# A two-layer decode step streamed through one 26 MB buffer: cache tiles of 4 MB, softmax rows turned in place, other places for the weights

## The chip, the cores and the metric

One core of a Trainium2 chip runs the kernel. Its engines are TensorE (PE), VectorE (DVE), ScalarE (ACT), GpSimd (POOL) and SyncE (SP), and 16 DMA engines bring data from the chip's main memory. The metric is the device time of one execution in microseconds (us); the kernel before took a median of 853.35 us in three runs (853.08 to 855.14).

## What is computed

Two transformer layers for one new token of each of 8 batches, in float32. Both layers use the same weights and the same caches:

```python
x = A_x                                    # (8, 1, 1024)
for layer in range(2):
    x = x + attention(layernorm(x))        # q = x @ wq: 32 heads of 128
    x = x + mlp(layernorm(x))              # gelu(x @ w1 + b1) @ w2 + b2, 3584 hidden
# attention: 4 K/V heads, each for 8 query heads, 4096 cached positions:
# softmax(q @ k.T * 128 ** -0.5) @ v, all heads joined, @ wo
```

The K cache holds 8 MB for each batch and so does V (4 heads x 4096 positions x 128 x 4 bytes), which makes 128 MB that each layer reads. wq and wo are 16 MB each, w1 and w2 are 14 MB each.

## The kernel before, in words

**One buffer.** Nearly everything that comes from memory lands in one tile, the arena: 52 units of 1024 columns (SCW) over 128 partitions, which is 512 KB a unit and 26 MB in all. A transfer of k units takes k neighbouring units from a given place. Sizes and places below are in units: (8, 28) is a 4 MB transfer into units 28 to 35. A piece of the cache, the half of one K/V head's positions of one batch, is 2 units (1 MB), so a batch has 8 pieces of K and 8 of V.

**One queue.** All these transfers stand in the list `stream`, in the order in which they are wanted, and SP issues them in that order and no other (`pump`, L229; the issue is L236). The head of the list is issued when its units are free. `release` frees a tile's units after its last reader and pumps. In the built program the wait is SP's: the transfer waits until PE has finished the last matmul that read the old content of these units, and all later transfers stand behind it. The 16 DMA engines work such transfers off one after the other; each is cut into rows of one partition, so every engine carries a sixteenth of each. A tile is one transfer with one semaphore, so PE can start on a 4 MB tile only when all of it has landed.

**Layer 0.** Units 0 to 27 hold wq, 14 MB of which stay for layer 1 (`held`, pieces ("q", kt, u)); the last 2 MB go partly to PSUM (`park`) and to the tile `spare`, and 64 KB are fetched once more ("qe"). Units 28 to 47 are the ring for the caches: 20 units. For each batch, PE multiplies the queries with 8 pieces of K (`scores`, L512: 4 matmuls of 512 columns for a piece, which the profile counts as 8), DVE scales the result into a row and takes maxima (L517), `probs` (L526 to L535) makes the exponentials on ACT, `turn` (L544 to L550) transposes them on PE, and `values` (L568) multiplies them with 8 pieces of V, after which `heads` (L580) joins each K/V head's result. PE does this in order: no V piece before its batch's softmax. The row of a batch and its transposed form S lie in the two units OWN = 50, 51 (`arena.own`).

**From layer 0 to layer 1.** The last 6 of the 8 pieces of batch 7's V stay in the arena, since layer 1 starts with batch 7 (`kept`). Then wo (`project`, L351), w1 (`expand`, L264, with `hidden_group` turning each group of h) and w2 (`swap`, L388) are streamed. wo and w1 of layer 0 go 4 units at a time through three places of 4 units (BLOCK_AT). In `swap`, w2 is multiplied in four column blocks c, and after each block two kt of wq, kept in units 0 to 27, make layer 1's queries (L299) and free their units. All of w2 but its last 4 of 28 kt in each block stays, in 24 units, for layer 1.

**Layer 1.** The batches go from 7 down to 0, with the 28 units that w2 leaves. At its end wo, w1 and the missing w2 are streamed again.

What sets the order is thus written by hand: sizes and places in the lists at L706 to L733. A place that is used again soon makes its transfer wait for PE.

Of the kernel before, what the change touches and what calls it, by code (L numbers as in the profile page):

```python
# [15 lines left out]
B, D = 8, 1024  # L16
HQ, HKV, SK, DH = 32, 4, 4096, 128
REP = HQ // HKV
F = 3584
# [34 lines left out]
class Arena:  # L54


    def __init__(self, ap):
        self.ap = ap
        self.freed = dict.fromkeys(range(N_UNIT), 0)
        self.clock = 0  # L60
        self.limit = OWN[0][0]
        self.own_at = OWN[0]

# [9 lines left out]
    def own(self):  # L73
        return self.take(1, self.own_at)

# [29 lines left out]
def decode_layers(ctx: ExitStack, tc: tile.TileContext, x, kc, vc, wq, wo, w1, w2, out):  # L105
# [123 lines left out]
    def pump():  # L229
        while stream:  # L230
            key, k, src, starts, keys = stream[0]
            slot = arena.take(k, [i for i in starts if i + k <= arena.limit])
            if slot is None:
                return
            stream.pop(0)
            nc.sync.dma_start(out=slot.ap[:, 0:src.shape[1]], in_=src)  # L236
            slot.cols = src.shape[1]
            slot.keys = keys
            held[key] = slot
# [155 lines left out]

    def arrive(c, kind):
        kts = W2_KTS[kind]
        slot = held[f"w2u{st['layer']}" if kind == "u" else "w2", c, *(() if kind == "u" else (kind,))]
        for e, kt in enumerate(kts):
            w2_at[c, kt] = slot.ap[:, e * Q4:(e + 1) * Q4]  # L400
        return list(kts)

    def swap():

        ys = small_ps("s")
        down(ys[:, 0:Q4], 0, arrive(0, 0), 0)
        flush()
# [13 lines left out]
        for c in range(CB):  # L421
            y = ys[:, c % 2 * Q4:(c % 2 + 1) * Q4]
            kts = []
            for kind in W2_ORDER[c]:
                kts += arrive(c, kind) if c or kind != 0 else []
            down(y, c, kts, NFT - len(kts))
            release(held.pop(("w2u0", c)))
            ysb = row_s[:, c % 2 * Q4:(c % 2 + 1) * Q4]
# [9 lines left out]
            for kt in (2 * c, 2 * c + 1):  # L438
                for u in range(2):
                    if kt < NT - 1:  # L440
                        late.append(lambda kt=kt, u=u: used(kt, u))
                        if (kt, u) != (3, 1):
                            late.pop()()
                    elif u == 0:
                        spot = st.pop("unparked")
                        q_part(acc, u, kt, 0, spot.ap)
                        spot.free()
                    else:
                        slot = held.pop(("qe", 0))
                        q_part(acc, u, kt, 0, slot.ap[:, 0:W - KEEP])  # L450
# [104 lines left out]
    def totals(b):  # L555
        pl = small_ps("pt")
        nc.tensor.matmul(pl[:, 0:HQ], ones, dl_s[b % 2], start=True, stop=True)
        nc.vector.reciprocal(rl_s[b % 2], pl[:, 0:HQ])
        st.pop(("row", b)).free()

# [86 lines left out]
    def unpark():  # L647
        spot = st.pop("spot")
        slot = arena.take(2, OWN[1][0:1])
        nc.scalar.activation(slot.ap, spot, AF.Copy)  # L650
        return slot
# [35 lines left out]
    any_of = lambda *at: lambda k, i: at  # L687

    def fixed(*at):
        return lambda k, i: (at[i],)  # L690

    def down_weights(c, layer, *spots):
        for kind, at in zip(W2_ORDER[c] if layer == 0 else "u", spots):
            key = (f"w2u{layer}", c) if kind == "u" else ("w2", c, kind)
            k0, k1 = (c * NFT + e for e in (W2_KTS[kind][0], W2_KTS[kind][-1] + 1))
            stream.append((key, (k1 - k0) // 4, w2[0][:, k0 * Q4:k1 * Q4], (at,), ()))

# [4 lines left out]
    def batch(layer, b, k_spots, v_spots):  # L702
        for a, spots in (("k", k_spots), ("v", v_spots)):
# [13 lines left out]
    i, j, k = LAST_BLOCKS  # L717
    down_weights(0, 0, i, j, j + 3)
    down_weights(1, 0, k, j + 2, 0)
    down_weights(2, 0, 2, 6, 1)  # L720
    down_weights(3, 0, 0, 8, 12)
    qe = (("qe", 0), 1, wq[0][:, -W:-KEEP], (1,), ())
    stream.append(qe)
    batch(1, last_b, ((4, 16), (4, 20), (4, 24), (2, 0), (2, 16)), ((4, 18),))
    batch(1, last_b - 1, ((2, 22), (4, 24), (2, 0), (2, 16), (4, 18), (2, 36)), ((8, 40), (8, 16)))
    cycle = [(((4, 24), (8, 36), (4, 44)), ((12, 16), (4, 36))), (((8, 40), (4, 16), (4, 20)), ((4, 24), (12, 36))),
             (((12, 16), (4, 36)), ((8, 40), (8, 16)))]
# [3 lines left out]
    weights(("i1",), w1[0], [4] * 6 + [2, 2], fixed(40, 44, 16, 20, 24, 36, 40, 42))  # L731
    for c in range(CB):
        down_weights(c, 1, 44 + c)  # L733
    pump()
    rs = layernorm(x_row, rsum)
    queries(rs)
    for layer in range(2):
        st["layer"] = layer
        b2_row = spare[:, 0:Q4]
        hooks = {("turn", last_b): opened} if layer == 0 else {  # L740
            ("v", *v_at(last_b - 2, 0)): lambda: bias_row(b2_row, spare[:, Q4:Q4 + CH]),
            ("v", *v_at(last_b - 1, 1)): rebuild}
# [7 lines left out]
        else:  # L750
# [24 lines left out]
            for c in range(CB):  # L775
                arrive(c, "u")
            grow(W2_KTS["u"], range(CB - 1))
            grow(W2_KTS["u"], (CB - 1,))
            nc.vector.tensor_tensor(x_row, x_row, y[0], ALU.add)
# [70 lines left out]
```

## Time and profile before

| | us |
|---|---|
| median of 3 runs (range) | 853.35 (853.08 to 855.14) |
| the profiled execution's own time | 854.68 |
| its span, first to last instruction | 852.9 |
| PE busy in it | 542.3 |
| DVE busy | 204.2 |
| ACT busy | 73.6 |

The queue of SP carries 358.82 MB, in 135 loads and one store. A row of the chain of waits gives a start, a length and what was worked or waited on; a DMA row in it begins with the issue of the transfer and ends when its tile has landed. A row of the timeline is start, duration, engine, line, operation and shapes, the count, and in brackets how long the engine had been idle before it and for what. PEclk is the clock granted to TensorE as a share of full speed. In a table of windows "DMA share" is the mean busy share of the 16 DMA engines.

### The profile page before, as it was taken

To read this page: it belongs to the slowest core of one execution; us is meant where nothing else is said; L and a number is where in the kernel's file an instruction comes from. 1 tells how busy PE (TensorE), PEld (TensorE's weight loads), DVE (VectorE), ACT (ScalarE), POOL (GpSimd) and SP (SyncE) were. 2 spreads that over 40 slices of the span, in tenths; PEclk is the share of its full clock that TensorE was granted. 3 is DMA by queue.
4 is the path that set the end of the run, shared out by engine and by line. 5 is a ranking of instruction groups with operands and counts; after the bars stand their busy time and mean duration, and the time that the engine had idled before them with its cause. 6 is when DMAs were issued, how large, how long until landed. Compare 5 with 4: busy or idle time off the path is not lost.

```text
span 852.9 us, 9923 instructions
## 1 busy us (share of the span) xinstructions
PE 542.3 (64%) x4226; PEld 190.8 (22%) x4226; DVE 204.2 (24%) x758; ACT 73.6 (9%) x164; POOL 1.7 (0%) x13
## 2 busy tenths in 40 slices
PE   0746665675765656655787786647557465474788
PEld 0212121121211121222233232111212111121344
DVE  0012231322222122300420242223223122231034
ACT  0110000000000000001311100000000000000042
POOL 0000000000000000000000000000000000000000
PEclk9977767776678777787889987858688777786889
DMA  9999999999999999999999999999999999999995
GB/s 400 417 442 417 438 427 436 422 440 420 429 428 431 433 435 424 426 427 428 423 388 407 416 433 422 438 425 445 434 419 424 434 425 443 423 425 442 415 426 241
DMA packets 19772, 359.60 MB, mean 422 GB/s; under 512 B 2192, under 2 KB 2576, under 8 KB 3600
## 3 DMA queue, kind: packets, MB, share of 16 engines
q1 hardware_dynamic: 19584, 358.82, 98.8%
q8 instruction: 33, 0.54, 0.3%
q10 hardware_dynamic: 144, 0.15, 0.1%
q14 instruction: 11, 0.09, 0.0%
HBM read 358.83 MB, written 0.13 MB: 421 GB/s over the span
## 4 chain that ended last, share of the span: by engine, by line
DMA 70%; PE 25%; DVE 2%; issue 1%; ACT 1%; another core or an unknown queue 1%; SPq 0%; ACTq 0%; DVEq 0%
DMA arena<-in_k_dram 27%; DMA arena<-in_v_dram 22%; DMA arena<-in_wo_dram 8%; DMA arena<-in_w_dram 8%; PE sps L512 7%; PE o_ps L568 7%; DMA arena<-in_wq_dram 5%; PE acc L264 2%; PE y L351 2%; PE sps L394 2%; PE sps L388 1%; PE acc L299 1%; PE sps L544 1%; PE sps L284 1%
## 5 line engine op out<-in xcount | busy, mean ns | idle before, releaser
L568 PE MATMUL o_ps<-arena 128*32 128x512 f32 x1024 | 166.9, 777 | 81.3 <-DMA arena<-in_v_dram 81.3
L512 PE MATMUL sps<-arena,qz 128*32 128x512 f32 x1024 | 152.2, 737 | 95.4 <-DMA arena<-in_k_dram 95.1
L512 PEld LDWEIGHTS sps<-arena,qz 128*32 128x32 f32 x1024 | 32.9, 127 | 179.5 <-DMA arena<-in_k_dram 95.8
L573 DVE SCALAR_TENSOR_TENSOR scr<-o_ps,bits,scr 128x128 f32<-128x128 f32 x192 | 67.4, 351 | 6.8
L535 ACT ACTIVATE arena<-arena,bits 128x512 f32<-128x512 f32 x32 | 22.8, 714 | 526.0 <-DVE scr L530 526.0
L568 PEld LDWEIGHTS o_ps<-arena 128*32 128x32 f32 x1024 | 33.6, 131 | 145.9 <-issue 110.0
L571 DVE TENSOR_SCALAR scr<-o_ps,bits 128x128 f32<-128x128 f32 x64 | 22.4, 351 | 171.1 <-PE o_ps L568 171.1
L351 PE MATMUL y<-arena,oxT 128*32 128x256 f32 x512 | 38.9, 459 | 32.0 <-DMA arena<-in_wo_dram 32.0
L517 DVE TENSOR_SCALAR_CACHE_REDUCE arena<-sps 128x512 f32<-128x512 f32 x32 | 22.1, 692 | 148.5 <-PE sps L512 148.5
L544 PE MATMUL sps<-ident,arena 128*128 128x128 f32 x128 | 29.3, 392 | 24.5 <-ACT arena L535 24.3
L264 PE MATMUL acc<-arena,oxT 128*32 128x256 f32 x448 | 35.4, 455 | 10.2 <-DMA arena<-in_w_dram 10.2
L580 PEld LDWEIGHTS sps<-bits,scr 128*128 128x128 f32 x128 | 21.7, 213 | 68.2 <-issue 40.1
L299 PE MATMUL acc<-arena,oxT 128*32 128x512 f32 (+1 forms) x250 | 32.1, 649 | 5.6 <-DMA arena<-in_wq_dram 4.1
L351 PEld LDWEIGHTS y<-arena,oxT 128*32 128x32 f32 x512 | 17.7, 127 | 51.5 <-DMA arena<-in_wo_dram 37.3
L581 DVE TENSOR_TENSOR oxT<-sps,scr 128x8 f32<-128x8 f32 x64 | 10.5, 164 | 72.8 <-PE sps L580 72.8
L544 PEld LDWEIGHTS sps<-ident,arena 128*128 128x128 f32 x128 | 21.2, 196 | 29.5 <-ACT arena L535 29.3
L580 PE MATMUL sps<-bits,scr 128*128 128x8 f32 x128 | 27.6, 288 | 0.0
L526 PE MATMUL sps<-scr,bits 128*128 128x128 f32 x32 | 7.7, 322 | 22.8 <-DVE scr L522 22.8
L264 PEld LDWEIGHTS acc<-arena,oxT 128*32 128x32 f32 x448 | 14.8, 125 | 22.7 <-DMA arena<-in_w_dram 9.7
L388 PE MATMUL sps<-arena,oxT 128*32 128x256 f32 x224 | 16.4, 423 | 4.2 <-DMA arena<-in_w_dram 4.2
L548 DVE COPY arena<-sps 128x512 f32<-128x512 f32 x16 | 11.1, 692 | 30.6 <-PE sps L544 30.6
L394 PE MATMUL sps<-arena,oxT 128*32 128x256 f32 x224 | 16.6, 394 | 0.8 <-DVE oxT L341 0.5
(109 smaller groups left out, 229.0 us busy)
## 6 DMA issues: line engine op xcount, KB each, us to landing
arena<-in_v_dram SPq DMA_DIRECT2D x19, 4096.0 KB, 18.9
arena<-in_k_dram SPq DMA_DIRECT2D x31, 2048.0 KB, 17.0
arena<-in_k_dram SPq DMA_DIRECT2D x12, 4096.0 KB, 18.7
arena<-in_w_dram SPq DMA_DIRECT2D x17, 2048.0 KB, 12.1
arena<-in_v_dram SPq DMA_DIRECT2D x4, 6144.0 KB, 25.6
arena<-in_v_dram SPq DMA_DIRECT2D x11, 2048.0 KB, 20.6
arena<-in_wo_dram SPq DMA_DIRECT2D x10, 2048.0 KB, 12.6
arena<-in_k_dram SPq DMA_DIRECT2D x2, 6144.0 KB, 23.5
```

The lines of the kernel that those rows point to most:

```text
L264: nc.tensor.matmul(acc[32 * j:32 * j + 32, 0:G], xnT[:, kt * XS:kt * XS + 32], slot.ap[:, c:c + G], start=(kt < 4), stop=(kt >= NT - 4))
L299: nc.tensor.matmul(acc[u][32 * j:32 * j + 32, d0 - j * CH:d1 - j * CH], xnT[:, kt * XS:kt * XS + 32], ap[:, d0 - c0:d1 - c0], start=(kt == ...
L351: nc.tensor.matmul(y[32 * j:32 * j + 32, 0:Q4], lhs[:, n * B:n * B + 32], slot.ap[:, c + j * Q4:c + (j + 1) * Q4], start=(n == 0), stop=(n ...
L388: nc.tensor.matmul(y[32 * g:32 * g + 32], h_at(kt), w2_at[c, kt], start=(n < 4), stop=(n >= NFT - 4))
L394: nc.tensor.matmul(y[32 * c:32 * c + 32], h_at(kt), w2_at[c, kt], start=(kt == 0), stop=(kt == NFT - 1))
L512: nc.tensor.matmul(ps[32 * g:32 * g + 32, :], qz[:, c:c + 32], kt[:, g * CH:(g + 1) * CH], start=(j == 0), stop=(j == HKV - 1))
L535: nc.scalar.activation(part, part, AF.Exp, bias=bias, scale=1.0, accum_out=ls[:, h:h + 1])
L544: nc.tensor.transpose(pp[:, t * P:(t + 1) * P], row[:, c:c + P], ident)
L568: nc.tensor.matmul(o[32 * g:32 * g + 32, :], s[:, g], v[:, g * CH:(g + 1) * CH], start=(half == 0), stop=(half == NH - 1))
L571: nc.vector.tensor_scalar(r, o[:, 0:P], sel_t[:, 0:1], None, op0=ALU.mult)
L573: nc.vector.scalar_tensor_tensor(r, o[:, t * P:(t + 1) * P], sel_t[:, t:t + 1], r, op0=ALU.mult, op1=ALU.add)
L580: nc.tensor.matmul(po[:, 0:REP], r_s[j % 2], sel_h, start=True, stop=True)
```

## The change

- **Rows turned in place.** `turn` writes S over the row itself, half by half, so one unit is enough: OWN is unit 51. In layer 1 that row lies in `spare` (`own_ap`), behind the 64 KB of wq that go to x_row now ("qe", with k = 0: no units).
- **7 of 8 pieces of batch 7's V stay**, so layer 1 loads one piece (1 MB) less.
- **4 MB cache tiles.** In layer 0, batches 1 to 6 load K as two tiles of 8 units and V as 4, 8 and 4 units. Both 4-unit tiles of V use units 44 to 47. In layer 1, batches 5 to 0 use 8-unit tiles alone, through three places (24, 32, 16).
- **10 places for wo and w1 of layer 0** (units 42 to 51): wo in tiles of 5 and 4 units by turns at 46 and 42, w1 in tiles of 4, 2 and 4 at 42, 50 and 46. Before it was three places of 4 units.
- **w2 in other parts** (W2_PARTS: kt and place); the last group of h is turned before w2 is begun (`swap` flushes first).

```diff
@@ constants
 N_UNIT = 52
-OWN = (50, 51), (14, 15)
-BLOCK_AT = 28, 32, 48
-LAST_BLOCKS = 28, 32, 48
+OWN = N_UNIT - 1
+UNPARK = 16
...
-W2_KTS = {0: range(16), 1: range(16, NFT - 4), "u": range(NFT - 4, NFT)}
-W2_ORDER = (0, 1, "u"), (0, 1, "u"), (0, 1, "u"), ("u", 0, 1)
+LAST = NFT - 4
+W2_PARTS = (((8, 48), (16, 42), (4, 50)), ((4, 51), (8, 46), (8, 0), (8, 2)),
+            ((4, 50), (16, 4), (8, 8)), ((4, 51), (16, 10), (8, 14)))
+LATE_AT = 40, 41, 50, 51
@@ class Arena
-        self.limit = OWN[0][0]
-        self.own_at = OWN[0]
+        self.limit = OWN
+        self.own_ap = None
...
     def own(self):
-        return self.take(1, self.own_at)
+        return self.take(1, (OWN,)) if self.own_ap is None else Kept(self.own_ap)
@@ def pump
-            slot = arena.take(k, [i for i in starts if i + k <= arena.limit])
+            if not k:
+                slot = Kept(starts)
+            else:
+                slot = arena.take(k, [i for i in starts if i + k <= arena.limit])
@@ def swap
         ys = small_ps("s")
-        down(ys[:, 0:Q4], 0, arrive(0, 0), 0)
         flush()
...
-            kts = []
-            for kind in W2_ORDER[c]:
-                kts += arrive(c, kind) if c or kind != 0 else []
-            down(y, c, kts, NFT - len(kts))
-            release(held.pop(("w2u0", c)))
+            n = 0
+            for i in range(len(W2_PARTS[c])):
+                kts = arrive(("w2", c, i), w2_kts(c, i))
+                down(y, c, kts, n)
+                n += len(kts)
+            release(held.pop(("w2", c, [m for m, _ in W2_PARTS[c]].index(4))))
...
-        arena.own_at = OWN[1]
+        arena.own_ap = spare[:, 0:SCW]
@@ def turn
         row = st["row", b].ap
-        st["S", b] = arena.own()
+        st["S", b] = st.pop(("row", b))
@@ def totals
-        st.pop(("row", b)).free()
@@ the lists of transfers
-    n_kept = 6
+    n_kept = 7
...
-    cycle = [(((8, 32), (4, 40), (4, 44)), ((8, 28), (8, 36))), (((4, 44), (8, 28), (4, 36)), ((8, 40), (8, 28))),
-             (((8, 36), (4, 44), (4, 28)), ((8, 32), (8, 40))), (((8, 28), (4, 36), (4, 40)), ((4, 44), (8, 28), (4, 36))),
-             (((8, 40), (4, 28), (4, 32)), ((8, 36), (4, 44), (4, 28)))]
-    for n, b in enumerate(orders[0][:-1]):
-        batch(0, b, *cycle[n % 5])
-    batch(0, last_b, ((8, 36), (4, 44), (4, 28)), ((4, 32), (8, 36), (4, 44)))
-    blocks = any_of(*BLOCK_AT)
-    weights(("o0",), wo[0], [4] * 8, blocks)
-    weights(("i0",), w1[0], [4] * (F // CH), blocks)
...
+    batch(0, 0, ((8, 36), (4, 44), (4, 32)), ((4, 28), (8, 36), (4, 44)))
+    for b in orders[0][1:-1]:
+        a, e = (28, 36) if b % 2 else (36, 28)
+        batch(0, b, ((8, a), (8, e)), ((4, 44), (8, a), (4, 44)))
+    batch(0, last_b, ((8, 28), (8, 36)), ((2, 44), (8, 28), (6, 36)))
+    weights(("o0",), wo[0], [5, 4, 5, 4, 5, 4, 5], fixed(46, 42, 46, 42, 46, 42, 46))
+    weights(("i0",), w1[0], [4, 2, 4, 4, 2, 4, 4, 2, 2], fixed(42, 50, 46, 42, 50, 46, 42, 50, 46))
...
-    qe = (("qe", 0), 1, wq[0][:, -W:-KEEP], (1,), ())
+    stream.append((("qe", 0), 0, wq[0][:, -W:-KEEP], x_row[:, 0:W - KEEP], ()))
-    batch(1, last_b, ((4, 16), (4, 20), (4, 24), (2, 0), (2, 16)), ((4, 18),))
-    batch(1, last_b - 1, ((2, 22), (4, 24), (2, 0), (2, 16), (4, 18), (2, 36)), ((8, 40), (8, 16)))
+    batch(1, last_b, ((4, 18), (2, 22), (4, 24), (2, 16), (2, 50), (2, 18)), ((2, 20),))
+    batch(1, last_b - 1, ((4, 22), (2, 26), (6, 16), (4, 28)), ((8, 32), (8, 16)))
...
-    for n, b in enumerate(orders[1][2:]):
-        batch(1, b, *cycle[n % 3])
-    weights(("o1",), wo[0], [4, 12, 8, 4, 2, 2], fixed(24, 36, 16, 24, 36, 38))
+    at = [24, 32, 16] * (4 * B)
+    for b in orders[1][2:]:
+        batch(1, b, *([(8, at.pop(0)), (8, at.pop(0))] for _ in "kv"))
+    weights(("o1",), wo[0], [8, 8, 8, 4, 2, 2], fixed(24, 32, 16, 24, 28, 30))
...
-        b2_row = spare[:, 0:Q4]
+        b2_row = spare[:, SCW:SCW + Q4]
```

The first place is SP's queue in layer 0, batches 1 and 2; 128x8192 is a tile of 8 units (4 MB), 128x4096 one of 4. Before:

```order
L236 DMA arena<-in_k_dram 128x4096
L236 DMA arena<-in_k_dram 128x8192
L236 DMA arena<-in_k_dram 128x4096
L236 DMA arena<-in_v_dram 128x8192 x2
L236 DMA arena<-in_k_dram 128x8192
L236 DMA arena<-in_k_dram 128x4096 x2
L236 DMA arena<-in_v_dram 128x8192 x2
```

After:

```order
L240 DMA arena<-in_k_dram 128x8192 x2
L240 DMA arena<-in_v_dram 128x4096
L240 DMA arena<-in_v_dram 128x8192
L240 DMA arena<-in_v_dram 128x4096
L240 DMA arena<-in_k_dram 128x8192 x2
L240 DMA arena<-in_v_dram 128x4096
L240 DMA arena<-in_v_dram 128x8192
L240 DMA arena<-in_v_dram 128x4096
```

K comes in two tiles instead of three, V in three instead of two; the two small V tiles share their place.

The second place is the same queue at the end of layer 0: the last cache tiles, wo, and the start of w1 (in_w stands for w1 and w2). Before:

```order
L236 DMA arena<-in_k_dram 128x4096 x2
L236 DMA arena<-in_v_dram 128x4096
L236 DMA arena<-in_v_dram 128x8192
L236 DMA arena<-in_v_dram 128x4096
L236 DMA arena<-in_wo_dram 128x4096 x8
L236 DMA arena<-in_w_dram 128x4096 x8
L236 DMA arena<-in_w_dram 128x2048
L236 DMA arena<-in_w_dram 128x1024
```

After:

```order
L240 DMA arena<-in_v_dram 128x2048
L240 DMA arena<-in_v_dram 128x8192
L240 DMA arena<-in_v_dram 128x6144
L240 DMA arena<-in_wo_dram 128x5120
L240 DMA arena<-in_wo_dram 128x4096
L240 DMA arena<-in_wo_dram 128x5120
L240 DMA arena<-in_wo_dram 128x4096
L240 DMA arena<-in_wo_dram 128x5120
L240 DMA arena<-in_wo_dram 128x4096
L240 DMA arena<-in_wo_dram 128x5120
L240 DMA arena<-in_w_dram 128x4096
L240 DMA arena<-in_w_dram 128x2048
```

The eight equal tiles of wo became seven of 5 and 4 units, and w1 got tiles of 2 units between those of 4.

The third place is PE at the start of `swap`: L284 (after: L288) turns groups of h, L388 (L392) is w2, L433 (L443) turns the block's result, and L299 (L303) is a kept piece of wq. Before:

```order
L264 MATMUL acc<-arena,oxT 32x256 x8
L284 MATMUL sps<-ident,scr 128x128 x2
L388 MATMUL sps<-arena,oxT 32x256 x16
L284 MATMUL sps<-ident,scr 128x128 x2
L388 MATMUL sps<-arena,oxT 32x256 x12
L433 MATMUL sps<-bits,scr 128x8 x2
L299 MATMUL acc<-arena,oxT 32x512 x16
```

After:

```order
L268 MATMUL acc<-arena,oxT 32x256 x8
L288 MATMUL sps<-ident,scr 128x128 x4
L392 MATMUL sps<-arena,oxT 32x256 x28
L443 MATMUL sps<-bits,scr 128x8 x2
L303 MATMUL acc<-arena,oxT 32x512 x16
```

The last turn of h moved ahead of the 16 matmuls of w2 that stood before it, and the block's 28 matmuls are one run.

More of the change, by code (lines that the diff above doesn't have):

```diff
@@ L394, in down_row, with w2_kts, arrive @@
                 nc.tensor.matmul(y[32 * c:32 * c + 32], h_at(kt), w2_at[c, kt], start=(kt == 0), stop=(kt == NFT - 1))
-    def arrive(c, kind):
-        kts = W2_KTS[kind]
-        slot = held[f"w2u{st['layer']}" if kind == "u" else "w2", c, *(() if kind == "u" else (kind,))]
+    def w2_kts(c, i):
+        if W2_PARTS[c][i][0] == 4:
+            return range(LAST, NFT)
+        k0 = sum(n for n, _ in W2_PARTS[c][:i] if n > 4)
+        return range(k0, k0 + W2_PARTS[c][i][0])
+    def arrive(key, kts):
+        slot = held[key]
         for e, kt in enumerate(kts):
-            w2_at[c, kt] = slot.ap[:, e * Q4:(e + 1) * Q4]
-        return list(kts)
+            w2_at[key[1], kt] = slot.ap[:, e * Q4:(e + 1) * Q4]
+        return kts
     def swap():
         ys = small_ps("s")
-        down(ys[:, 0:Q4], 0, arrive(0, 0), 0)
         flush()
@@ L449, in swap @@
                         slot = held.pop(("qe", 0))
[L450 removed]
+                        q_part(acc, u, kt, 0, slot.ap)
                         q_part(acc, u, kt, W - KEEP, spare)
@@ L648, in unpark @@
         spot = st.pop("spot")
-        slot = arena.take(2, OWN[1][0:1])
+        slot = arena.take(2, (UNPARK,))
         nc.scalar.activation(slot.ap, spot, AF.Copy)
@@ L734, in decode_layers @@
+    for c in range(CB):
+        down_weights(("late", c), c, range(LAST, NFT), LATE_AT[c])
     pump()
```

30 lines of the change are left out of this document (10 added, 20 removed).

## Prediction

> **What bounds the kernel now.** I read the page's line of the DMA engines and its chain, then a table of windows, then the chain row by row.
>
> ```profile
> DMA  9999999999999999999999999999999999999995
> DMA 70%; PE 25%; DVE 2%; issue 1%; ACT 1%; another core or an unknown queue 1%; SPq 0%; ACTq 0%; DVEq 0%
> ```
>
> ```profile
> core 0: us, PE busy (x) PEld busy (x) DVE busy (x) ACT busy (x) POOL busy (x), PEclk, DMA share, GB/s
> 100.00:340.00 240.00, 154.46 (x928) 47.51 (x920) 59.27 (x201) 12.70 (x30) 0.00 (x0) 0.73 1.00 430
> ...
> 580.00:760.00 180.00, 108.13 (x690) 33.29 (x686) 44.63 (x153) 10.59 (x25) 0.00 (x0) 0.76 1.01 431
> ```
>
> The DMA engines are full from start to end, at 430 GB/s. The time is the bytes at that rate plus whatever lets the engines run dry. PE is busy less than two thirds of the time; it counts only through the places it frees: if SP issues a transfer after the one ahead of it has landed, or shortly before, the engines idle and nothing makes that up later. So each part of the change is asked two things: how many bytes, and is a place free in time. At 430 GB/s one unit (0.524 MB) takes 1.22 us, 4 units 4.88, 8 units 9.75.
>
> **What a late issue costs.** The engines start some time after an issue. Three places bound that:
>
> ```profile
> 0.74 2.02 SPq L236 DMA_DIRECT2D arena<-in_wq_dram  x4
> arena<-in_wq_dram SPq DMA_DIRECT2D x1, 22.1
> ...
> 850.25 0.35 SPq L781 DMA_DIRECT2D out_dram<-xb  x1
> out_dram<-xb SPq DMA_DIRECT2D x1, 128.0 KB, 1.7
> ...
> 443.89 0.33 SPq L236 DMA_DIRECT2D arena<-in_w_dram  x1
> arena<-in_w_dram SPq DMA_DIRECT2D x1, 512.0 KB, 3.9
> 445.72 0.33 SPq L236 DMA_DIRECT2D arena<-in_w_dram  x1
> arena<-in_w_dram SPq DMA_DIRECT2D x1, 2048.0 KB, 9.2
> ```
>
> The first tile, 8 MB, landed 22.1 us after its issue into idle engines; its bytes take 8.39 MB / 430 = 19.5, so 2.6 are dead. The store of 128 KB took 1.7, with 0.3 for its bytes: 1.4. In `swap` a tile issued at 443.89 landed at 447.8; the next, issued at 445.72, landed at 454.9, 7.1 later instead of 4.88: 2.2 lost though it was issued 2.1 ahead, 4.3 together. I take 2.6 us, from the row most like a cache tile (a load, MBs, empty engines); 1.4 and 4.3 are the ends.
>
> **The bytes.** One piece of V less: 1.05 MB / 430 GB/s = -2.4 us. The 64 KB of wq are still fetched.
>
> **The 4-unit tile of V used twice (layer 0, batches 1 to 6).** The order is K1 (8), K2 (8), V1 (4, at 44), V2 (8), V3 (4, at 44 again). V3 waits for V1's two pieces, these for the batch's softmax, and that for all of K2. Let K2 land at 0. V1 and V2, already queued, land by 4.88 + 9.75 = 14.63; then the engines have only V3. How long do K2, softmax and V1 take?
>
> ```profile
> 170.40 3.64 PE L512 MATMUL sps<-arena,qz 128*32 128x512 f32 x16 [3.61 <-DMA arena<-in_k_dram]
> ...
> 209.42 3.64 PE L512 MATMUL sps<-arena,qz 128*32 128x512 f32 x16 [5.62 <-DMA arena<-in_k_dram]
> 213.00 0.53 PE L580 MATMUL sps<-bits,scr 128*128 128x8 f32 x2
> 213.45 2.89 PE L512 MATMUL sps<-arena,qz 128*32 128x512 f32 x24
> ```
>
> After an idle stretch of 3.6 to 5.6 us the first two pieces (x16) take 3.64, the next 0.96 each (2.89 for three). Windows beside the first row say why:
>
> ```profile
> 168.94:172.35 3.41, 1.95 (x12) 0.59 (x16) 0.00 (x0) 0.00 (x0) 0.00 (x0) 0.50 0.95 404
> 172.35:175.76 3.41, 3.41 (x18) 0.90 (x14) 0.17 (x1) 0.00 (x0) 0.00 (x0) 0.50 1.03 437
> 175.76:179.18 3.42, 3.12 (x28) 0.60 (x20) 0.70 (x2) 0.00 (x0) 0.00 (x0) 0.95 1.01 431
> ```
>
> PEclk is 0.50 until PE has been busy for a whole such window, then 0.95. In the new layout PE idles in the same way ahead of K2: it ends K1 5.6 us after its landing and waits some 4 for K2. So K2 takes 3.64 + 2 x 0.96 = 5.56. The rest is in the chain of batch 3:
>
> ```profile
> 180.20 2.04 PE sps L512 x16
> 182.26 0.71 DVE arena L517 x2
> ...
> 187.42 2.88 PE o_ps L568 x16
> 190.30 0.07 PE sps L557
> 190.37 19.00 DMA arena<-in_k_dram
> ```
>
> From the last score at 182.24 to V's first matmul at 187.42 pass 5.18; two pieces of V and the release of their place take 2.95 more, to the issue at 190.37. Turning the row in place changes none of it: `turn` already ends half a row's transposes before it writes, and the row's next writer comes after the batch's last V. So V3 is issued at 0.04 + 5.56 + 5.18 + 2.95 = 13.7, 0.9 ahead of V2's landing, and 2.6 - 0.9 = 1.7 us are lost, six times: +10.2. K1 of the next batch then queues at once, so nothing is made up. The ends:
>
> ```profile
> 135.33 3.77 PE sps L512 x32
> ...
> 112.13 3.68 PE o_ps L568 x16
> ```
>
> With PE at full clock throughout, K2 takes 3.77 and V1 2.04 (the 180.20 row): 11.0, and no loss. All at half clock, K2 7.28 and V1 3.68: 16.2, and 4.2 lost each time. Before, no small V tile reused the place of another of its batch.
>
> **wo and w1 in 10 places.** With two places by turns, a 5-unit tile of wo can be issued only when the 5-unit tile before it is used up, and only the 4-unit tile between covers that: 4.88 us. Use of a 4-unit tile:
>
> ```profile
> 362.12 1.99 PE y L351 x32
> ...
> 376.71 3.17 PE y L351 x32
> ...
> 391.39 3.37 PE y L351 x32
> ```
>
> Their mean, 2.84, times 5/4 is 3.55: 3.55 + 2.6 - 4.88 = 1.3 lost, for the second to fourth 5-unit tile and for w1's first tile at 50, which waits for the last of them behind a 4-unit tile: four times, +5.1 (0 with 1.99 and 1.4; 2.1 each with 3.37, and 3.8 with 4.3 dead as well). The 4-unit tiles have 5 units (6.1 us) of cover against 3.4, and so have the later tiles of w1: hidden. Before, three places gave two tiles, 9.8 us, of cover.
>
> **w2.** In the change, w2's second block goes to units that the first pieces of wq free, and only 3 units (0.5 and 1 MB, 3.66 us) are queued ahead of that transfer once block 0's last tile has landed.
>
> ```profile
> 439.28 2.09 PE sps L388 x24
> ...
> 441.40 0.44 DVE scr L429
> ...
> 442.76 3.80 PE acc L299 x29
> ```
>
> Block 0's last 4 kt (a third of 2.09: 0.7), copy, turn and add (441.40 to 442.76: 1.36), and the first piece of wq (8 of 29 in 3.80: 1.05) make 3.2 with the start: 3.2 + 2.6 - 3.66 = 2.1 lost. The kernel before loses 2.2 in the same stretch, as shown above: net 0 (-2.2 to +1.7, for no loss and for 4.3 dead). That h's last group is turned first delays w2's first matmuls by under 1 us; block 0's last tile lands 7 units, 8.5 us, after w1's last one, so that is hidden.
>
> **Layer 1.** Batch 6's 6-unit tile waits for the one V piece that batch 7 loads. From that piece's landing: a last K piece at half clock 1.8 + softmax 5.18 + one V piece at half clock 1.8, less the 2.44 by which K landed earlier, 6.4; cover is 6 units, 7.3: 6.4 + 2.6 - 7.3 = +1.7 (0 to 3.4). From batch 5 on all tiles have 8 units and three places; the tightest is V1, whose place is taken up to 7.28 + 5.18 + 7.28 = 19.7 us after K2's landing, while three tiles queued behind K2 last 29.3: hidden, with 7 us beyond the dead time. The end of the program loads the same tiles of w1 and w2 as before; its wo tiles wait for places freed long before.
>
> **Do larger tiles move faster?** Layer 0's mix of 2 and 4 MB ran at 430 GB/s, layer 1's with tiles up to 6 MB at 431: worth at most 2 us over the whole, and I take 0. The Trainium skill (Perfetto Trace Analysis, DMA Optimizations) says that larger DMA sizes use memory bandwidth better; by that rule this change gains, but these rows show no more left to gain. The Trainium skill (DMA: Bandwidth & Descriptors, Anatomy of one DMA) gives a fixed cost of about 2.0 us a transfer, for the path from GpSimd; with 2.0 in place of 2.6 the sum below would be +7.1, an estimate, and the trace's 1.4 to 4.3 neither confirms nor excludes it.
>
> **The sum.** -2.4 + 10.2 + 5.1 + 0 + 1.7 = +14.6 us. The profiled execution took 854.68 for a span of 852.9, 1.3 above the median of 853.35; carried over to the median it is 853.35 + 14.6 = 868.
>
> **Rivals.** (a) *No place is late; only the bytes count.* V1 is used up before 14.63 - 2.6 = 12.0 us after K2's landing, as it would be with PE at full clock (11.0), and wo's 5-unit tiles within 2.3. Then 853.35 - 2.4 = 851, or 849 if the 2.2 in `swap` go as well. For it: the two full-clock rows. Against: after every idle stretch shown, two pieces ran at half clock. 10%. (b) *The waits are there but small*, because dead time is nearer 1.4: 6 x 0.5 for V3, 0.1 x 4 for wo, 0.5 in layer 1, w2 1.2 better, -2.4: 854, no change that can be told. For it: the store's row. Against: the two loads. 12%. (c) *The clock makes it worse.* Each loss lengthens PE's idle stretch, and K2, V1 and wo all run at half clock: 6 x 4.2 + 4 x 1.9 (5/4 of 3.37) + 1.7 - 2.4 = +32, 885. For it: 0.50 ahead of K tiles; against: 0.95 comes back within two pieces. The Trainium skill (TensorE: Matmul & The Clock Gate, HAM oscillation) describes this: a wait for data longer than a window of about 3.4 us makes the next tile start at half clock, every time; the rows agree. 13%.
>
> **Chances and range.** My forecast has 65%, with 856 to 880 for itself: V3 at 0.8 to 3, wo at 0 to 2. The limit for telling a change from none is 0.3%, 2.6 us. Slower: 65 + 13 and half of (b), 84%; same: 8%; faster: 8%. The range is 855 to 881: below it lie (a) and part of (b), above it most of (c).
>
> **What would show it.** In layer 0's batches 1 to 6 a K tile of 4 MB, then V3's issue 13 to 15 us after K2's landing; a dip in DMA share before each V3, some 1 to 3 us, and none in batch 0 or in layer 1 from batch 5 on; the chain with more PE between DMA rows; wo's 5-unit tiles issued 1 to 2 us ahead of the landing before them. I am wrong if V3 is issued by 12 us after K2, or if engines flow within 1 us of an issue.

## The result, and the profile after

The changed kernel takes 889.07 us, median of six runs (886.47 to 891.63), against 853.59 (852.21 to 855.14) for the kernel before, measured beside it: a ratio of 1.0417, 95% interval 1.0394 to 1.0439. It is 35.5 us slower. The prediction said slower, by 14.6, and its range ended at 881: the sign was right, the size was not.

The page of the kernel after, the DMA line of the 40 slices and the chain by engine:

```profile
DMA  9999999989998999988997999999999999999996
DMA 65%; PE 29%; DVE 3%; issue 2%; another core or an unknown queue 1%; ACT 0%; SPq 0%; DVEq 0%; ACTq 0%
```

The eights and sevens are new: the DMA engines run dry in layer 0, and the chain passes through PE more often. The table of windows of the kernel after (columns as in the prediction: the engines' busy times, PEclk, DMA share, GB/s) says in which stages:

```profile
100.00:340.00 240.00, 146.74 (x854) 45.73 (x854) 57.87 (x197) 12.70 (x30) 0.00 (x0) 0.77 0.94 396
345.00:445.00 100.00, 60.00 (x562) 23.06 (x558) 16.98 (x72) 9.76 (x23) 0.00 (x0) 0.78 0.92 380
445.00:510.00 65.00, 47.51 (x498) 18.98 (x489) 13.44 (x68) 8.77 (x20) 0.12 (x1) 0.84 0.90 364
580.00:760.00 180.00, 120.20 (x704) 37.92 (x696) 46.14 (x154) 10.58 (x25) 0.00 (x0) 0.77 1.00 431
```

The two middle rows of the kernel before:

```profile
345.00:445.00 100.00, 67.32 (x682) 27.36 (x682) 23.93 (x115) 13.58 (x35) 0.12 (x1) 0.77 1.00 420
445.00:510.00 65.00, 52.27 (x494) 19.23 (x486) 17.02 (x60) 7.51 (x11) 0.00 (x0) 0.93 1.00 413
```

Layer 0's caches moved at 430 GB/s before and move at 396 now; in the stretches with wo, w1 and w2, 380 and 364 GB/s are moved where it was 420 and 413. From layer 1's batch 5 on the queue is full again, at 431, as forecast. So the three places that the prediction named are the three that lose. They lose more than it said.

How much each loses can be read from the issue and the landing of every transfer. I call *lead* the time from a transfer's issue to the landing of the one ahead of it, and *loss* its landing less that one's landing, less its bytes at 429.5 GB/s. With a full queue a 4 MB tile lands 9.72 us behind the one ahead, and its loss is 0.

```
V3 of batch               1     2     3     4     5     6
issue after K2's landing  13.8  13.9  15.7  13.7  15.8  15.0   (mean 14.7; forecast 13.7)
lead                       0.8   2.6  -1.0   1.0  -1.2   1.0
loss                       1.3   1.7   3.5   2.5   3.4   1.2   (sum 13.6)
loss of a later transfer   1.4   -     1.1   -     1.3   0.9   (sum 4.8; leads of 6.6 to 17 us)

stage                      forecast    losses in the trace
V3, batches 1 to 6           +10.2     13.6 + 4.8 = 18.4
wo, w1                        +5.1     2.0 + 3.3 + 2.0 + 2.1, later 1.4 + 0.4 = 11.0
w2                             0       4.3 + 1.2 + 2.0 + 1.5 + 0.5 = 9.5; before 2.2 + 1.6 = 3.8
layer 1's start               +1.7     2.5 + 0.8 = 3.3; before 0.4
bytes                         -2.4     -2.4
```

The sum of the right column is 39.8; less what the kernel before lost as well, 3.8 in w2, 0.4 at layer 1's start and 1.2 in one transfer among the caches, it is +34.4; the profiled spans differ by 886.2 - 852.9 = 33.3.

One V3 at close range, batch 3 of the kernel after: first the chain from K2's landing at 185.11; then, of the DMA view, the packets that start from 196.5 to 197.5, the 8 us from 198 on in 40 slices of 0.2 (a packet counts in the slice in which it starts) with their packets, and the issue of V3.

```profile
185.25 6.48 PE sps L522 x32
...
195.18 1.97 PE sps L554 x8
197.15 3.68 PE o_ps L577 x16
200.83 0.02 issue
200.85 0.33 SPq L240
```

```profile
DMA packets 15, 0.03 MB, mean 33 GB/s; under 512 B 14, under 2 KB 14, under 8 KB 14
...
DMA  0300000000000000000992024998995995995997
...
DMA packets 100, 1.62 MB, mean 203 GB/s; under 512 B 2, under 2 KB 2, under 8 KB 2
...
arena<-in_v_dram SPq DMA_DIRECT2D x1, 2048.0 KB, 7.3
```

The packets under 512 B have 4 bytes. Each transfer ends with 16 of them, which I read as one from each DMA engine. Fourteen of V2's come by 197.2, the other two at 198.9 and 199.5, and V2 lands at 199.8: most engines are idle 2.6 us before the landing. SP issues V3 at 200.85. Its first packets start 1.0 later, at 201.8, and take up to 1.6 us, where later ones take 0.61. V3 lands 7.3 after its issue, where 4.88 would be its bytes. The K2 tile took 6.48 (forecast 5.56) and V1 3.68 (forecast 2.95): the half clock that the prediction ended after two pieces of K2 lasts longer here.

### The profile page after: what moved, and what is told of

It reads as the page before. It is cut to its first block, busy times and chain, and to the rows that moved or that the text cites. A ratio compares the mean times of both kernels' runs of the same rounds, so it can differ in the third digit from the quotient of the medians.

```text
span 886.2 us, 9973 instructions
## 1 busy us (share of the span) xinstructions
PE 564.0 (64%) x4226; PEld 197.7 (22%) x4226; DVE 204.4 (23%) x758; ACT 73.4 (8%) x164; POOL 1.7 (0%) x13
## 4 chain that ended last, share of the span: by engine, by line
DMA 65%; PE 29%; DVE 3%; issue 2%; another core or an unknown queue 1%; ACT 0%; SPq 0%; DVEq 0%; ACTq 0%
DMA arena<-in_k_dram 28%; DMA arena<-in_v_dram 16%; PE sps L522 9%; DMA arena<-in_wo_dram 8%; DMA arena<-in_w_dram 8%; PE o_ps L577 8%; DMA arena<-in_wq_dram 5%; PE y L355 2%; PE acc L268 2%; PE acc L303 2%; PE sps L398 1%; PE sps L392 1%; PE sps L554 1%; PE sps L288 1%; PE sps L589 1%
## 5 line engine op out<-in xcount | busy, mean ns | idle before, releaser
L522 PE MATMUL sps<-arena,qz 128*32 128x512 f32 x1024 | 175.4, 832 | 136.1 <-DMA arena<-in_k_dram 135.1
L577 PE MATMUL o_ps<-arena 128*32 128x512 f32 x512 | 81.5, 763 | 21.9 <-DMA arena<-in_v_dram 21.4
L577 PE MATMUL o_ps<-arena,spare 128*32 128x512 f32 x512 | 79.3, 738 | 16.1 <-DMA arena<-in_v_dram 15.9
L303 PE MATMUL acc<-arena,oxT 128*32 128x512 f32 x248 | 35.4, 717 | 5.4 <-DMA arena<-in_wq_dram 3.9
L545 ACT ACTIVATE arena<-arena,bits 128x512 f32<-128x512 f32 x16 | 11.4, 714 | 291.0 <-DVE scr L540 291.0
L545 ACT ACTIVATE spare<-spare,bits 128x512 f32<-128x512 f32 x16 | 11.4, 714 | 254.5 <-DVE scr L540 254.5
L577 PEld LDWEIGHTS o_ps<-arena 128*32 128x32 f32 x512 | 15.7, 126 | 53.8 <-issue 36.3
L577 PEld LDWEIGHTS o_ps<-arena,spare 128*32 128x32 f32 x512 | 16.3, 124 | 45.5 <-issue 35.5
L392 PE MATMUL sps<-arena,oxT 128*32 128x256 f32 x224 | 16.5, 438 | 9.2 <-DMA arena<-in_w_dram 9.2
L554 PE MATMUL sps<-ident,spare 128*128 128x128 f32 x64 | 14.0, 378 | 12.3 <-ACT spare L545 12.2
## 6 DMA issues: line engine op xcount, KB each, us to landing
arena<-in_w_dram SPq DMA_DIRECT2D x14, 2048.0 KB, 12.1
```

Of the source, the lines that this page charges most:

```text
L303: nc.tensor.matmul(acc[u][32 * j:32 * j + 32, d0 - j * CH:d1 - j * CH], xnT[:, kt * XS:kt * XS + 32], ap[:, d0 - c0:d1 - c0], start=(kt == ...
L392: nc.tensor.matmul(y[32 * g:32 * g + 32], h_at(kt), w2_at[c, kt], start=(n < 4), stop=(n >= NFT - 4))
L522: nc.tensor.matmul(ps[32 * g:32 * g + 32, :], qz[:, c:c + 32], kt[:, g * CH:(g + 1) * CH], start=(j == 0), stop=(j == HKV - 1))
L545: nc.scalar.activation(part, part, AF.Exp, bias=bias, scale=1.0, accum_out=ls[:, h:h + 1])
L554: nc.tensor.transpose(pp[:, t * P:(t + 1) * P], row[:, c:c + P], ident)
L577: nc.tensor.matmul(o[32 * g:32 * g + 32, :], s[:, g], v[:, g * CH:(g + 1) * CH], start=(half == 0), stop=(half == NH - 1))
```

## Experiments

Twelve kernels, in four groups. The kernel before ran beside each group: 852.4, 852.6, 852.9 and 853.7 us. Theory 1 is the prediction's: a place that comes free late leaves the engines dry. Theory 2: big tiles, few places and a half clock cost by themselves. Theory 3 came up in the traces: what a dry stretch costs behind it.

**1. Other places for layer 0's K and V.**

```
-        a, e = (28, 36) if b % 2 else (36, 28)
-        batch(0, b, ((8, a), (8, e)), ((4, 44), (8, a), (4, 44)))
+    ring = [(((8, 28), (8, 36)), ((4, 44), (8, 28), (4, 36))), (((8, 40), (8, 28)), ((4, 36), (8, 40), (4, 28))),
+            ...
+        batch(0, b, *ring[b - 1])
```

> Changed: only the places of layer 0's batches 1 to 6. The 4 MB K tiles stay where the ring allows, V's small tile never gets the place of another small tile of its batch; all else as in the changed kernel (889.1 us). Theory 1 (a place freed late leaves the engines dry): the six late issues ahead of V3 go, worth in the changed kernel's trace about 3.0 us each, 18 in all; one late place stays, ahead of batch 7's first K tile, about 2.8: 874 us (872 to 876). By the prediction's own 1.7 us for each: 889.1 - 10.2 + 1.7 = 881. Theory 2 (4 MB tiles and a PE at half clock cost by themselves, wherever the places are): 886 or more.

Measured: 871.45 us, 1.0231 of before (1.0201 to 1.026), 17.6 below the changed kernel; by the profiled spans (886.2 and 869.3) 16.9. The first row of its windows:

```profile
100.00:340.00 240.00, 146.43 (x900) 45.27 (x904) 58.20 (x198) 12.70 (x30) 0.00 (x0) 0.80 1.00 427
```

The DMA share is 1.00 at 427 GB/s, with 4 MB tiles and with PE at 0.80. Theory 2 falls for the caches. The one late place that is left (K1 of batch 7) had a lead of 2.44 us in this trace and lost 0.17: together 2.6, the dead time of the prediction. The gain is about 3 us for each V3, not 1.7.

**2. wo and w1 in tiles of 2 units, in the same 10 places.**

```
-    weights(("o0",), wo[0], [5, 4, 5, 4, 5, 4, 5], fixed(46, 42, 46, 42, 46, 42, 46))
-    weights(("i0",), w1[0], [4, 2, 4, 4, 2, 4, 4, 2, 2], fixed(42, 50, 46, 42, 50, 46, 42, 50, 46))
+    weights(("o0",), wo[0], [2] * 16, fixed(*(42, 44, 46, 48) * 4))
+    weights(("i0",), w1[0], [2] * 14, fixed(42, 44, 50, 46, *(48, 42, 44, 50, 46) * 2))
```

> Changed: only the tiles of layer 0's wo and w1, 2 units each (1 MB) in the same 10 places in place of 5 and 4 units by turns. Theory 1: each issue then waits for 2 units and is covered by 6 to 8 others; the losses of wo and w1 in the changed kernel's trace, about 11 us, go: 878 us (876 to 881). By the prediction's term of 5.1 us: 884. Theory 2 (the 10 places are too few whatever the tiles are, or small tiles move slower): 889.

Measured: 874.84 us, 1.0253 (1.0236 to 1.027), 14.2 below the changed kernel; by the profiled spans (886.2 and 874.3) 11.9. Its windows:

```profile
345.00:445.00 100.00, 70.08 (x636) 25.02 (x628) 22.27 (x101) 13.06 (x33) 0.00 (x0) 0.77 1.01 421
```

No transfer of wo or w1 loses more than 0.06 us, and the least lead is 5.3. Ten places are enough; two tiles of half of them by turns are not.

**3. PE kept busy.**

```
+        def busy(n):
+            z = ps_o.tile([P, CH], F32, tag="o", name="z")
+            for i in range(4 * n):
+                nc.tensor.matmul(z[32 * (i % 4):32 * (i % 4) + 32, :], qz[:, 0:32], spare[:, 0:CH], ...)
+        idle = {("k", 0, 3): 5, ("k", 1, 3): 1, "probs": 2, ("v", 1, 0): 3, ("v", 1, 3): 7}
```

> Added: matmuls of 128x512 on data that lie ready, into a psum tile that nobody reads, in layer 0's batches 1 to 6 where PE waits (20 behind K1, 4 behind K2, 8 behind the softmax, 12 behind V1, 28 behind V3); they keep TensorE's granted clock up. Places and transfers as in the changed kernel. Theory 1 with the clock as a cause of the lateness: K2 is used in 3.8 us and V1 in 2.0, V3 is issued 11 to 12 us after K2's landing in place of 14.7, and no more than 0.5 us of the 3.0 is lost each time: 871 to 875 us. If the half clock has no part in it: 889, or more by the added matmuls.

Measured: 872.90 us, 1.0244 (1.0218 to 1.0271), 16.2 below the changed kernel though it does 432 matmuls more (the profile counts each twice). First row of the windows, then the chain of batch 3, whose K2 landed at 182.95:

```profile
100.00:340.00 240.00, 209.28 (x1748) 65.86 (x1740) 58.51 (x200) 12.70 (x30) 0.00 (x0) 0.97 0.99 420
```

```profile
183.28 3.48 PE sps L522 x32
...
191.99 1.92 PE o_ps L577 x16
193.91 0.06 PE sps L567
193.97 9.91 DMA arena<-in_v_dram
```

The clock is 0.97 in place of 0.77. V3 is issued 11.0 us after K2 in batches 3 to 6 (12.1 and 12.7 in the first two), with leads of 3.6 to 5.1. So the places are too few *at half clock*; at 0.97 the same places come free 2 to 4 us earlier and in time. The Trainium skill (TensorE: Matmul & The Clock Gate, HAM oscillation) says that a PE that waits for data longer than its window starts every tile at half clock; both traces agree, 0.77 and 0.97. Some 5 us of loss stay all the same, 1.0, 1.1, 1.3 and 1.5 us in transfers whose leads were 3.8 to 10 us. They are the matter of runs 9 and 10. In the traces the losses among the caches fall from 18.4 to 6.9 us; another 4 us of the gain are in wo and w1, where no matmul was added, and why is open.

**4. The conflict alone, in the kernel before.**

```
+    for b in orders[0][1:6]:
+        a, e = (28, 36) if b % 2 else (36, 28)
+        batch(0, b, ((8, a), (8, e)), ((4, 44), (8, a), (4, 44)))
+    batch(0, 6, ((8, 36), (8, 28)), ((4, 44), (4, 36), (8, 28)))
+    batch(0, last_b, ((4, 40), (4, 44), (4, 36), (4, 28)), ((4, 32), (8, 36), (4, 44)))
```

> The kernel before (853.6 us) with one part of the change alone: layer 0's batches 0 to 5 get the changed kernel's tiles and places (4 MB K tiles, V's 4-unit tile twice at 44); batches 6 and 7 are laid out with places that come free early; n_kept, wo, w1, w2, softmax rows and layer 1 as before. Five late issues of V3. Theory 1: 5 x 3.0 = +15, 868.6 us (866 to 871). By the prediction's 1.7 each: +8.5, 862. Theory 2 (the loss in the changed kernel needs its other parts, too): 853 to 858.

Measured: 867.15 us, 1.0168 (1.0153 to 1.0183): +14.7 for five late V3, 2.9 each. Nothing else of the change is needed for it. Lead and loss of the five add up to 2.30, 2.30, 2.33, 3.54 and 2.33 us: a dead time of 2.3, once with 1.2 more. The other losses of that stretch, 1.3, 0.9, 1.0 and 1.6, fall on transfers whose lead was 6.8 us or more.

**5 to 7. The repairs together.** Runs 1 and 2 in one kernel; then also w2's first 16-kt tile as two of 8; then also layer 1's 6-unit tile as 4 and 2 units.

```
-W2_PARTS = (((8, 48), (16, 42), (4, 50)), ...
+W2_PARTS = (((8, 48), (8, 42), (8, 44), (4, 50)), ...
```
```
-    batch(1, last_b - 1, ((4, 22), (2, 26), (6, 16), (4, 28)), ...
+    batch(1, last_b - 1, ((4, 22), (2, 26), (4, 16), (2, 20), (4, 28)), ...
```

> Both repairs together: the ring of places for layer 0's K and V of the first run of this study, and the 2-unit tiles of wo and w1 of the second. If the two losses are separate things, the gains add: 889.1 - 17.6 - 14.2 = 857.3 us (855 to 860), with the loss in the w2 stretch (about 9 us in the trace, 4 to 5 of it more than before) and that of layer 1's start (2 to 3) left as they are. If one loss hides behind the other: 865 or more.

> As the kernel with both repairs, and w2's 16-kt tile of block 0 (at 42) is loaded as two of 8 kt (at 42 and 44); nothing else. In the changed kernel's trace 40 matmuls, 4.2 us at half clock, stand behind the landing of block 0's last two tiles, since the 16-kt tile lands only 1.2 us ahead of the 4-kt one. Theory 1: with 8-kt tiles 24 of them stand there or fewer, the first place of wq comes free 2 to 3 us earlier, and the loss ahead of w2's second block falls from 4 to 5 us to 1 to 3: 2 to 4 us below the run with both repairs, 853 to 855. If the chain from block 0 to wq is late for another reason: no difference to that run (within 1 us).

> As the one ahead of it, and the 6-unit K tile of layer 1's second batch (at 16) is loaded as one of 4 and one of 2 units, so that only 2 units wait for the place of the single V piece. Theory 1: its late issue (lead 0.3 us, 3.4 lost in the first run's trace) gets 4.9 us more of cover; 2 to 3.4 us less than the run ahead of it: 850 to 852 us, at or just below the kernel before (852 to 854). If layer 1's start loses nothing by that tile: the same as the run ahead of it.

Measured: 862.71 (1.0122, 1.009 to 1.0154), 862.89 (1.0111, 1.0075 to 1.0147) and 858.77 us (1.0077, 1.0051 to 1.0103). The first gains 26.4 where 31.8 was expected; by the profiled spans, 859.3 against 886.2, it is 26.9 of the 28.8 that runs 1 and 2 sum to. K1 of batch 7, the late place left by run 1, lost 0 to 0.3 us in three of the five profiles that have it and 2.3 and 3.6 in the others, so these kernels vary by that much from execution to execution.

The second is not as expected: cutting the tile brought nothing to the median, and the w2 stretch loses 8.7 us in its trace where the first run's loses 8.4. The chain of the changed kernel, and the same place in the second run, as its timeline has it, both from PE's start on block 0's last tiles to the piece of wq that frees a place:

```profile
467.18 4.19 PE sps L392 x40
471.37 0.02 issue
471.39 0.44 DVE scr L439
471.83 0.04 issue
471.87 0.63 PE sps L443 x4
...
472.75 1.97 PE acc L303 x16
```

```profile
443.68 2.79 PE L392 MATMUL sps<-arena,oxT 128*32 128x256 f32 x24 [0.55 <-DMA arena<-in_w_dram]
...
447.01 1.02 PE L443 MATMUL sps<-bits,scr 128*128 128x8 f32 x4 [0.55 <-DVE scr L439]
```

There are 24 matmuls behind the landing in place of 40, and they take 2.79 in place of 4.19, as expected. But what follows takes longer (the turn 1.02, not 0.63): the granted clock stays at 0.50 through it. The first place comes free 5.37 us after block 0's last landing, against 5.39 in the run without the cut. The third run has the same cut, and in its trace the clock is back at 1.00 from 444.1 on:

```profile
444.15 0.61 PE L443 MATMUL sps<-bits,scr 128*128 128x8 f32 x4 [0.55 <-DVE scr L439]
```

There the first place comes 4.10 us after block 0's last landing, and the transfer that waits for it loses 2.5 where the second run's loses 3.9. So the cut can gain 1.3 us; in the second run's trace the half clock took the gain.

The third is 4.1 us faster than the second, against 2 to 3.4 expected, but that can't be put down to the 6-unit tile alone. The tile lost 3.4 in the second run's trace and the tiles in its place lose nothing; yet K1 of batch 7 lost 0.3 in the third's trace for 3.6, and the two kernels' times overlap (859.79 to 865.22 and 858.43 to 863.39).

**8. Rows in place, alone.** In `turn`, `st["S", b] = st.pop(("row", b))` in the kernel before.

> The kernel before with one part of the change alone: softmax rows turned in place, so that one unit of its own is used and not two; all tiles and places as before. All theories, the prediction among them: no difference, 852 to 854.5 us. If turning in place holds up the transposes or the next batch's row: 856 or more.

Measured: 853.30 us, 1.0001 (0.9992 to 1.001). No cost, as forecast.

**9. More instructions for POOL.**

```
+    tick = bit(1)
+    for _ in range(2560):
+        nc.gpsimd.memset(tick, 0.0)
```

> The kernel before, with 2560 memsets of one column on POOL (which has nothing else to do there), from the program's start on; transfers, places and the other engines as before. They make POOL fetch about 10 more 16 KB blocks of instructions, each a packet of about 1.06 us on one of the 16 DMA engines, in a stretch where the queue is never short. Theory 3 (with a full queue a fetch only makes one engine lag, and an engine that lags costs time only when it is the one furthest behind, or after the queue ran dry and all start together): 853 to 855.5 us. Rival (each fetch holds up the transfer that it meets, wherever it falls): 10 x 1.06 to 1.3 more, 863 to 866.

Measured: 864.73 us, 1.0129 (1.0102 to 1.0155): +12. Theory 3 as it was written is wrong, and the rival's sum is right, though not its parts. A row of the windows of this run, then of the kernel before, over the stretch in which POOL runs its memsets; and two lines of this run's DMA view of the same stretch:

```profile
30.00:376.00 346.00, 214.14 (x1340) 68.19 (x1332) 80.59 (x271) 23.41 (x47) 218.80 (x2207) 0.77 1.00 421
```

```profile
30.00:376.00 346.00, 219.09 (x1400) 69.45 (x1392) 80.52 (x271) 23.29 (x47) 0.00 (x0) 0.75 1.00 429
```

```profile
q8 instruction: 11, 0.18, 0.2%
q14 instruction: 22, 0.18, 0.1%
```

The DMA share stays 1.00, no place is late (the least lead is 5.9 us), and yet 421 GB/s are moved instead of 429. POOL's instructions come through queue 14 in blocks of 8 KB, 22 here against 4 in the kernel before. From 70 us on, every 20 us, a transfer loses 0.6 us, 16 times up to 376: once for each of the 16 blocks that the memsets add there. So a fetch of instructions can delay the landings of a full queue, time after time.

**10. More instructions for PE.** The matmuls of run 3 in batches 1 to 6 of both layers of the kernel before.

> The kernel before, with matmuls on data that lie ready in batches 1 to 6 of both layers (72 of 128x512 a batch, into a psum tile that nobody reads); places and transfers as before. PE's instruction stream grows by 876 matmuls; the one of the warm run grew by 444 and had 40 blocks of 16 KB fetched in place of 33, so some 14 more blocks here, 47. Theory 3, in the form that the memsets on POOL left it: a fetch makes one DMA engine lag; fetches on one and the same engine add up (POOL: 0.61 us for each of 17), while PE's go round eight engines, so that with a full queue only each eighth costs (in the kernel before the 1st and the 9th cost 1.49 and 1.21 us, the 2nd to 8th nothing): 14/8 x 1.2 = +2, 854 to 857 us. Rival (each fetch costs its own 1.06): +15, 867. Rival (PE's fetches cost nothing): 852.5 to 853.5.

Measured: 857.83 us, 1.0056 (1.0034 to 1.0078), +5.0; 47 blocks on queue 8, as expected. +15 falls, and "nothing" falls; the +2 of theory 3 was low, since the interval begins at 2.9. What PE's fetches (queue 8, 16 KB, some 1.07 us each) cost is seen when the loss of the transfer that each one meets is listed in order:

```
PE's fetch number        1    2    3    4    5    6    7    8    9   10   16   17   24   25   32   33
kernel before          1.5    0    0    0    0    0    0    0  1.2    0  2.2* 1.6    0  0.3    0  0.8
before, w2 in halves   1.4    0    0    0    0    0  0.2    0  1.3    0    0  1.5    0  1.4    0  1.5
conflict alone (4.)    1.2    0    0  1.3  0.9  1.0  2.3*   0  1.6    0    0  0.8    0  1.6    0  1.6
kernel after           1.6    0    0  1.5    0  1.1  2.5*   0  1.3  0.9  1.2  1.5    0    0    0    0
0: under 0.15 us either way
* on a transfer whose lead was under 2.6 us
```

The second row (run 11) has no late place at all, and its losses stand at 1, 9, 17, 25 and 33: each eighth fetch costs, and nothing between. In the third row, between the five dry stretches, fetches 4, 5, 6 and 7 cost too. Run 10's own trace is less regular: up to the 22nd fetch its losses stand at 1, 9 and 17 (1.2, 0.5, 0.5), at 2, 10 and 18 (0.3, 0.4, 0.4) and at 6, 14 and 22 (0.8, 0.6, 0.7), eight apart again but split.

This fits theory 3 in its second form, and the 4-byte packets at the end of each transfer show it. In the kernel before, after PE's fetches 1 to 6, as many of the 16 come 1.5 to 2 us behind the first, and they stay so from transfer to transfer; after the eighth it is nine, with one that POOL's own fetches made late, and after the ninth a single one comes 3.4 us behind. So a fetch makes one engine lag, by some 1.5 us; with a full queue the lag stays, and the next seven fetches, on other engines, hide in it. A dry stretch starts all engines level again, and the next fetch costs its full lag: in the kernel after, the 16 ends lie 2.0 us apart at V2 of batch 1 and 0.4 at V3, behind the dry stretch; in batch 3, 2.6 and 0.7. POOL's fetches add up because they come to one engine: in run 9 the last of the 16 comes 0.8 us behind the one ahead of it at 74 us, and 3.2 us at 204.6. The trace does not name the engines; that each of the 16 packets stands for one is inferred.

The +5.0 is not all shown to be fetches. The profiled execution was the fastest of the four, 856.19 us, and its losses sum to only 1.3 more than in the trace of the kernel before; and one transfer's lead fell to 2.8 us there, from 10.3, and it lost 1.4. The other executions left no trace.

**11. w2's tiles by halves, in the kernel before.** Here, and in 12, `pump` issues two transfers for each w2 tile of layer 0.

> The kernel before with each of layer 0's w2 tiles loaded by two transfers of half its size into the same places, so that PE starts on a tile when half of it has landed; nothing else. Theory 1: the first place that wq frees in the w2 stretch comes 1 to 2 us earlier, the lead of the transfer that waits for it grows from 2.1 to 3 to 4 us, and its loss of 2.2 us goes or shrinks to 1: 850.5 to 852 us, 0.1 to 0.3% below the kernel before. If halves are slower to move, or PE's half clock takes the gain: 853 or more.

Measured: 853.06 us, 0.9996 (0.9986 to 1.0005), no difference. The transfer that lost 2.2 us loses nothing now. But without that dry stretch fetches 25 and 33 cost 1.4 and 1.5 us, where they cost 0.3 and 0.8: with the 1.5 of fetch 17 that is 4.4 us, against 4.9 for the same places before. One trace of each kernel shows this.

**12. All four repairs and w2 by halves, in the changed kernel.**

> The changed kernel with all four repairs: the ring of places, wo and w1 in 2-unit tiles, w2's 16-kt tile of block 0 and the 6-unit tile of layer 1 cut in two, and now also each of layer 0's w2 tiles loaded by two transfers of half its size. In the trace of the run without the last of these (858.8 us) the two stretches behind w2's blocks 0 and 1 lose 2.5 + 1.5 and 1.7 + 1.3 us. Theory 1: leads there grow by 1 to 1.5 us and the losses fall by as much each: 855 to 857 us, still above the kernel before, since with 10 places fewer units are queued there than with its 12. If all of both losses goes: 852. If nothing changes: 858 to 859.

Measured: 859.16 us, 1.0068 (1.0044 to 1.0091): nothing gained. In its trace the first place behind block 0 still came 1.15 us after the engines ran dry, and lost 3.5.

None of these versions beats the kernel before.

## Why the prediction was right and wrong

- *The engines are the bound, and a late place costs* was right. Undoing the two conflicts gives back 26.4 of the 35.5 us (run 5), and the first alone, in the kernel before, costs 14.7 (run 4).
- *Dead time 2.6* was right: 2.3 in run 4, 2.6 in run 1. The Trainium skill (DMA: Bandwidth & Descriptors, Anatomy of one DMA) has about 2.0 for another path; the measured numbers are a little higher, and the estimate from it would have been further off. (That estimate is written as +7.1; twelve places with 0.6 less each make it +7.4.)
- *V3: 13.7 us, 1.7 lost, six times, +10.2* had the right mechanism and the wrong size: 18.4 in the trace, 17.6 by run 1. The lateness itself was sized well. Issues came 14.7 us after K2, 1.0 later than worked out, most of it since V1 up to the issue took 3.5 to 3.7, nearly all at half clock, for 2.95 (K2 took 5.1 to 6.5, on average 5.6, for 5.56, and the stretch between 5.0 to 5.8, for 5.18); but V2 landed 15.2 after K2 on average, not 14.63, and the dead time was 2.3. With 2.3 less the lead, where that is positive, the six V3 lose 1.5, 0, 3.3, 1.3, 3.5 and 1.3, together 10.9. The step that failed is the end of the sum, "six times: +10.2 ... nothing is made up": it has no term for what a dry stretch costs behind it. The other 7.5 us are of that kind, single losses of 0.9 to 1.7 on transfers that meet a fetch or follow one that did: a dry stretch starts the engines level, so a fetch behind it is no longer hidden (runs 4 and 10).
- *wo and w1, +5.1*: 11.0. The step "their mean, 2.84, times 5/4 is 3.55" failed. The new kernel has PE waiting longer ahead of each 5-unit tile, and it uses all of it at half clock:

```profile
393.94 4.54 PE y L355 x40
```

  That is 1 us more for a tile; with a dead time of 2.3 the loss is 2.0, not 1.3, four times. Another 1.3 are in the one tile that lost 3.3, and 1.4 in a later transfer; both meet a fetch.
- *w2, net 0* was wrong: 9.5 against 3.8. The step that failed is "block 0's last 4 kt (a third of 2.09: 0.7)". I took from the kernel before what stands behind the last landing, but the changed kernel loads 16 kt in the last tile but one, which lands 1.2 us ahead of the last: 40 matmuls, 4.19 us, stand there. With it the chain is the 5.6 us of the trace, not 3.2. The second gap, behind block 1 (2.0 + 1.5), I did not look for. Runs 6 and 12 did not mend it, and run 7's trace loses 1.4 less behind block 0; what would mend it is open.
- *Layer 1's start, +1.7*: 2.5 for the tile named, 2.5 to 3.7 in other runs; in run 7's trace it is gone. The lead was 1.0, about as worked out (7.3 less 6.4); the tile meets a fetch.
- *Rows in place: nothing* (run 8: 1.0001), *larger tiles: 0* (427 GB/s in run 1, 431 in layer 1) and *nothing from batch 5 on* were right.
- Rival (c), the clock makes it worse, at 885, was nearest and had 13%. Its mechanism was there (run 3: with the clock up, the caches lose 11.5 us less); its sum was partly chance, since it priced V3 at 4.2 each, which is 3.0, and had nothing for w2.

## What to carry to other kernels

A place that is reused within one batch is as late as everything that is done between: count that time at the clock that PE has after the wait, which the change itself lengthens, and then keep a lead of the dead time (2.3 to 2.6 us here) and 1.5 to 2.5 more, by which most engines here were done ahead of a landing (in run 3 leads of 3.6 to 3.9 still lost 0.3 to 1.3, and one of 5.1 nothing). Cut tiles so that several are in flight: the same ten places lost 11 us with tiles of half of them and nothing with tiles of a fifth. And where a change touches what lands last ahead of a chain, work that chain out from the new order of tiles, not from the rows of the old one.

## What was not expected of the hardware

Fetches of instructions take part in the time of a kernel that is bound by DMA. PE's, 33 blocks of 16 KB here, cost 1.2 to 1.6 us at each eighth as long as the queue stays full, and up to that much after every dry stretch; 864 matmuls that are of no use (run 10) made 14 more blocks, and the kernel was 5.0 us slower, not all of it shown to be fetches. POOL's cost 0.6 us for each 8 KB: 2560 memsets of one column, on an engine with nothing else to do, made the kernel 12 us slower. And a dry stretch of 2.2 us, taken away, brought nothing (run 11), since, as its trace has it, the dry stretch had kept two later fetches from costing their full lag.
